# Token softmax sums as single rows, inverses spread over the partitions through DRAM, rows through Wo two segments late

## The chip, the cores and the metric

One core of a Trainium2 chip runs the whole program. The metric is device time in microseconds of one launch, inputs and outputs as the reference has them. Several runs are given by their median; the profile is one further execution, taken by the hardware profiler.

## The reference, cut to what matters

Four blocks follow each other: A, B, A, B, each added to the residual `x` of 2048 x 512. B is a gated MLP with a 2048 x 2048 mixing over tokens. A is a recurrent attention over 64 segments of 32 tokens, and it is where the change is:

```python
mem = mem0                                   # 8 rows
for s in range(n_seg):                       # 64 segments, 32 tokens each
    h = concatenate([mem, x_segment])        # 40 rows of 512
    q, k, v = (einsum('btd,dhe->bhte', h, W) for W in (Wq, Wk, Wv))   # 32 heads of 128
    scores = where(mask, q @ k.T * 128**-0.5, -1e9)
    o = softmax(scores) @ v
    o = einsum('bhte,hed->btd', o, Wo)
    mem = o[:, :8]                           # the next segment starts from these 8 rows
    outs.append(o[:, 8:])                    # 32 token rows
```

So the eight memory rows of a segment must have gone through projection, attention and Wo before the next segment's projections can begin. The 32 token rows of a segment are wanted by nothing in that loop.

## The kernel before

**Tiling.** The heads are put on the free side. Q and K are projected in two halves `r` of 16 heads, by matrix multiplications with only 32 stationary columns (the segment's 32 rows), four of which run side by side in the four 32-column groups of the array. Scores and their exponentials `E` are held as keys on partitions (two groups `g` of 64, in two variants per half `r`) and head and query on the free axis. The product with V (`pv`) then gives the output transposed, 128 channels on partitions, which is the stationary form that Wo needs.

**Softmax sums.** The exponentials are not divided. `pv` gives undivided outputs in `psO[r]`; the sums over keys come from multiplications with a matrix of ones, which puts each sum on all 128 partitions. `sums_ahead` and `sums_memory` do it for the 8 memory queries, `sums_tokens` for the 32 token queries into `psT`, 1024 numbers on each partition. ScalarE turns sums into inverses by Ln and Exp(-x). VectorE multiplies, straight from PSUM: `memory_out` for the memory queries, `tok_out` and `last_out` for the tokens.

**Wo with rows of two segments.** The stationary tile `uT` has 32 rows for each head: 24 token rows of the segment before and 8 memory rows of this one. `tok_out` writes 24 token rows of segment s into the `uT` of s+1; `last_out` keeps the last 8 in `oB`, which pass Wo later in a batch (`y_part`). `wo_pairs` writes into `px` (heads 0 to 17), `wo_rest` into `pw`, a corner of `psO[0]` (heads 18 to 31). `fold` and `build_hA` add them and transpose the memory rows into `hT` of the next segment; `store_o` stores the 24 token rows to `o_d`. After the last segment a final pass through Wo (L1290 to L1306) sends the rows that are still left.

**Order.** In A the order on TensorE, VectorE and ScalarE is the order of the source, written out by hand; each of these engines works strictly in that order. SyncE and GpSimd are ordered by a scheduler. TensorE's order in one segment, without what hides it:

```python
qk(0) qk(2) qk(1) qk(3) v_mm(0) scores(0) v_mm(1) scores(1)
fill() sums_ahead fill() pv(0) pv(1) sums_memory(1) sums_tokens
wo_pairs wo_rest fill()
```

`fill()` asks the generator `more` for one piece of work that is not part of the recurrence: `b_units` (projections of the last 8 rows of the next block's segments, six chunks for each block of four segments, cut into pieces of one, three and four k-tiles) or `y_part`. In the fourth segment of the first blocks there is none left. `run(copies)`, `run(turns)` and `run(adds)` issue what evicts such a piece. `prep_segment` copies small operands of a coming segment on GpSimd. `HALVED` gives for each segment how many k-tiles of `qk(3)`, `v_mm(0)` and `v_mm(1)` are issued as two matrix multiplications of 256 columns instead of one of 512.

**Buffers.** `att` is one PSUM tile of two banks, used in turn for `psQ`, `psS` and `psT`; `accA` holds the pieces, `accB` in turn `psm`, `psV`, `px`; `attO[0]` in turn `psK` and `psO[0]`, `attO[1]` is `psO[1]`.

Of the kernel before, what the change touches and what calls it, by code (L numbers as in the profile page):

```python
# [7 lines left out]
BF16 = mybir.dt.bfloat16  # L8
# [23 lines left out]
    "7900906005096002908070807070807080708070807080707080708070708071",  # L32
    "9060050968093111918080708070807070807070807080708070807080707080",
# [25 lines left out]
def _consts(ctx, tc, c, b_sp):  # L59
# [38 lines left out]
    for g in range(2):  # L98
        nc.vector.memset(half[64 * g:64 * g + 64, g, :], 1.0)
    bsp_bf = cp.tile([P, 16], BF16, name="bsp_bf")  # L100
# [8 lines left out]
    c.update(ident_bf=ident_bf, maskN=maskN, ones=ones, half=half)  # L109
# [380 lines left out]
def kernel(  # L490
# [32 lines left out]
    rows.vb_d = dram.tile([P, 8 * DH], BF16, name="vb_d")  # L523
    with tc.manual_schedule(engines=ORDERED):
# [148 lines left out]
def a_block(tc, c, rows, front, MV_in, RS_in, MV_out, RS_out, ahead, wo, S, first):  # L673
# [4 lines left out]
    maskN, ones, half = c["maskN"], c["ones"], c["half"]  # L678

    with ExitStack() as ctx:  # L680
# [14 lines left out]
        vsp = ctx.enter_context(tc.tile_pool(name="a_vs", bufs=2))  # L695
# [47 lines left out]
        KAr = [pers.tile([P, 2, 16, 32], BF16, name=f"KA{i}") for i in range(2)]  # L743
# [21 lines left out]
        copies, turns, adds = [], [], []  # L765
# [5 lines left out]
        def b_units(tb, early=0):  # L771
# [59 lines left out]
        def y_part(G, q, last=False):  # L831
# [9 lines left out]
            for k, _ in enumerate(wo_last(parts, pwB, last and q > 0)):  # L841
                if k in (0, 3):
                    yield
# [75 lines left out]
        def store_o(s, pw, t1):  # L919

            o_sb = wk.tile([P, P], F32, name="o_sb", bufs=1)
            nc.vector.tensor_tensor(out=o_sb[:], in0=pw, in1=t1[:], op=ALU.add)
            nc.sync.dma_start(o_d[SEG * (s - 1):SEG * s, :].rearrange("r (cg c) -> cg r c", cg=4), o_sb[:])

        def segment(s, fill, spare0, spare1, spare2, spare3, tail, loads):
# [3 lines left out]
            KA = KAr[s % 2]  # L929
# [75 lines left out]

            def sums_tokens(ps):
# [25 lines left out]
            def rview(r, lo, hi):  # L1032
                return Rt[:].rearrange("p g (r n q) -> p r g n q", r=2, q=32)[:, r, :, :, lo:hi]

# [6 lines left out]
            def tok_out(r):  # L1041
                nc.vector.tensor_tensor(out=hview(uT_nxt[:], r, 0, 24), in0=oview(r, 8, 32), in1=rview(r, 0, 24), op=ALU.mult)  # L1042

            def last_out(r):
                nc.vector.tensor_tensor(out=hview(oB, r, 8 * (s % 16), 8 * (s % 16) + 8), in0=oview(r, 32, 40), in1=rview(r, 24, 32), op=ALU.mult)

            psQ = att.tile([P, 2, 512], F32, name="psQ")
            r0, _, read = qk(0, psQ[:, 0, :])
            r2, mms, _ = qk(2, psQ[:, 1, :])
            other_bank(mms, read)  # L1050
# [26 lines left out]
            spare0()  # L1077

# [5 lines left out]
            Rt = segp.tile([P, 2, 512], F32, name="Rt", tag="Rt", bufs=1)  # L1084

            def token_factors(rs):
                nc.scalar.activation(out=Rt[:], in_=psT[:], func=ACT.Ln)  # L1087
                for r in rs:
                    rt = Rt[:, :, 256 * r:256 * r + 256]
                    nc.scalar.activation(out=rt, in_=rt, func=ACT.Exp, scale=-1.0)  # L1090
# [20 lines left out]
            sums_tokens(psT)  # L1111
            if ends_here:
                spare2()
                token_factors((1, 0))
            else:
                memory_out(1, sums[1])
            run(copies)
# [15 lines left out]
            if not ends_here:  # L1133
                token_factors((0, 1))
                run(turns)
                spare2()
            t1 = wk.tile([P, P], F32, name="t1", bufs=1)
            fold(px, cross, t1, None if ends_here else beside)
            if ends_here:
                fill()  # L1140
                for r in (1, 0):
                    tok_out(r)
                    last_out(r)
            if s + 1 < NSEG:
                build_hA(s + 1, pw, t1)
            if s > 0:
# [17 lines left out]
        if first:  # L1164
# [3 lines left out]
            for gen in (units, units1, units):  # L1168
                for _ in range(3):
# [15 lines left out]
        def values():  # L1185
            for u, n in ((units, 2), (units, 1), (units1, 2), (units1, 1), (units1, 2), (units1, 1)):
# [103 lines left out]
        ends = (uT[NSEG % 2], oBs[NB // 4 - 1][:, :, 96:128])  # L1290
        pw = accB.tile([P, 512], F32, name="pw")
        for n in range(H // 2):
            i = (n + H // 4) % (H // 2)
            for k in range(4):
                h = 2 * i + k % 2
                nc.tensor.matmul(pw[32 * k:32 * k + 32, :], lhsT=ends[k // 2][:, h, :], rhs=wo.head(h).rearrange("p (kt g el) -> p g kt el", kt=4, g=4),
                                 start=(n == 0), stop=(n == H // 2 - 1), tile_position=(0, 32 * k))
        o_sb = segp.tile([P, DM], F32, name="o_end", tag="Rt", bufs=1)
        nc.scalar.copy(o_sb[:], pw[:])
        for k in range(2):  # L1300
            o = o_sb[64 * k:64 * k + 32, :]
            nc.vector.tensor_tensor(out=o, in0=pw[64 * k:64 * k + 32, :], in1=o_sb[64 * k + 32:64 * k + 64, :], op=ALU.add)
            if k == 0:
                nc.gpsimd.dma_start(o_d[S - SEG:S - 8, :], o[0:24, :])
            else:
                nc.sync.dma_start(o_d[S - P:S, :].rearrange("(j r) c -> j r c", j=4)[:, 24:32, :], o)  # L1306
# [37 lines left out]
```

## Time and profile before

| | |
|---|---|
| runs (three) | 1616.52, 1618.78, 1620.8 us; median 1618.78 us |
| the profiled execution | 1620.98 us, span from the first to the last instruction 1619.3 us |
| granted TensorE clock | 0.997 |
| TensorE busy | 1572.9 us, 97% |
| VectorE busy | 1215.1 us, 75% |
| ScalarE busy | 1064.7 us, 66% |
| GpSimd busy | 286.4 us, 18% |
| A blocks | 29 to 690 us, 831 to 1482 us |

A line of the timeline has the start in us, the time until the end of the last instruction merged into it, engine, line, operation, output<-inputs, shapes and count; an idle time of the engine before it stands in brackets with what ended it. Ends of matrix multiplications are modelled, so a run of them is read by the distance of starts. A line of groups has count, then busy us, mean ns of one, then idle us of the engine before them and who ended it.

### The profile page before, as it was taken

The page shows a single profiled execution, that of the slowest core. Times are in us where ns is not written, and L with a number is a line of the kernel's source. Part 1 is how long each engine was busy: PE and PEld are TensorE (multiplying, and loading weights), DVE is VectorE, ACT ScalarE, POOL GpSimd, SP SyncE. Part 2 cuts the span into 40 slices and gives each one's busy share as a digit, 9 for nine tenths or more (in the row PEclk, how much of TensorE's full clock was granted, in tenths as well). Part 3 has the DMA queues.
Part 4 walks back from the last instruction along what each step waited for, and adds up shares of the span by engine and source line. Part 5 has one row for each costly group of instructions (what it writes and reads, how often), then busy time and mean ns, then how long its engine had stood idle before and what let it go on. Part 6 is the DMA issues. An engine that isn't in the chain of part 4 may idle for free.

```text
span 1619.3 us, 94188 instructions
## 1 busy us (share of the span) xinstructions
PE 1572.9 (97%) x42526; PEld 1000.3 (62%) x42526; DVE 1215.1 (75%) x3181; ACT 1064.7 (66%) x2277; POOL 286.4 (18%) x604
## 2 busy tenths in 40 slices
PE   5899999999999999999999999999999999999999
PEld 2566666666666666666656666666666666665565
DVE  4787777878888887884467777777888788877722
ACT  3677777777777777661047777777777777776400
POOL 5111111112211221320011111111121112214000
PEclk8999999999999999999999999999999999999999
DMA  9222122223322343297952221222333233526698
GB/s 370 68 44 45 45 43 44 44 43 81 85 47 44 86 92 72 88 189 151 212 168 50 49 47 47 47 47 47 73 90 72 48 73 92 88 62 174 141 190 170
DMA packets 261851, 148.44 MB, mean 92 GB/s; under 512 B 196425, under 2 KB 238001, under 8 KB 261449
## 3 DMA queue, kind: packets, MB, share of 16 engines
q1 hardware_dynamic: 248184, 98.59, 28.9%
q0 software_dynamic: 12976, 42.77, 8.7%
q8 instruction: 333, 5.46, 1.5%
q10 hardware_dynamic: 288, 1.05, 0.2%
q14 instruction: 70, 0.57, 0.1%
HBM read 59.42 MB, written 36.93 MB: 60 GB/s over the span
## 4 chain that ended last, share of the span: by engine, by line
PE 90%; DMA 4%; DVE 3%; ACT 1%; issue 1%; POOL 0%; SPq 0%; DVEq 0%
PE psQ L731 13%; PE psK L731 13%; PE psb L731 9%; PE pg L398 9%; PE px L808 9%; PE psm L731 7%; PE psV L731 6%; PE psO L815 6%; PE pz L298 3%; PE psO L1020 3%; PE pwB L827 3%; PE py L441 3%; PE psT L1012 2%; PE psS L968 2%; PE psO L1003 1%; PE psO L1023 1%
## 5 line engine op out<-in xcount | busy, mean ns | idle before, releaser
L731 PEld LDWEIGHTS <-hT 128*32 128x32 bf16 x14172 | 372.6, 96 | 284.6 <-DVE hT L917 65.5
L945 DVE STREAM_TRANSPOSE QQ<-rows 128x512 bf16<-128x512 bf16 x256 | 179.7, 702 | 19.5 <-ACT rows L942 11.9
L945 DVE STREAM_TRANSPOSE KA<-rows 128x512 bf16<-128x512 bf16 x256 | 176.4, 689 | 13.1 <-ACT rows L942 12.4
L398 PE MATMUL pg<-z,wspT 128*128 128x344 bf16 x1024 | 154.3, 309 | 0.0
L942 ACT CAST rows<-psQ 128x512 bf16<-128x512 f32 x256 | 142.2, 584 | 17.8 <-PE psQ L731 16.8
L1042 DVE TENSOR_TENSOR uT<-psO,Rt 128x384 bf16<-128x384 f32 x256 | 141.5, 553 | 13.6 <-ACT Rt L1090 5.9
L1090 ACT ACTIVATE Rt<-Rt 128x512 f32<-128x512 f32 x256 | 147.2, 622 | 4.1
L977 ACT ACTIVATE S<-psS 128x224 bf16<-128x224 f32 x256 | 91.4, 357 | 84.6 <-PE psS L972 84.6
L731 PE MATMUL psQ<-Wq_sb,hT 128*32 128x512 bf16 x2048 | 135.4, 381 | 9.0 <-ACT Rt L1087 6.3
L1039 DVE TENSOR_TENSOR uT<-psO,Rm 128x128 bf16<-128x128 f32 x252 | 73.4, 291 | 93.3 <-ACT Rm L1038 50.4
L808 PEld LDWEIGHTS <-uT 128*32 128x32 bf16 x4608 | 111.6, 96 | 47.2 <-DVE uT L1039 33.7
L808 PE MATMUL px<-Wo,uT 128*32 128x256 bf16 x3840 | 134.5, 274 | 2.1 <-DVE uT L1039 1.9
L731 PE MATMUL psV<-Wv_sb,hT 128*32 128x256 bf16 (+1 forms) x2420 | 134.3, 346 | 1.5 <-issue 1.5
L731 PE MATMUL psQ<-Wk_sb,hT 128*32 128x512 bf16 x2048 | 134.9, 381 | 0.0
L1087 ACT ACTIVATE Rt<-psT 128x1024 f32<-128x1024 f32 x128 | 131.0, 1024 | 5.5 <-PE psT L1012 2.5
L731 PE MATMUL psK<-Wk_sb,hT 128*32 128x512 bf16 (+1 forms) x2832 | 134.6, 320 | 0.0
L731 PE MATMUL psK<-Wv_sb,hT 128*32 128x512 bf16 (+1 forms) x2776 | 134.5, 323 | 0.0
L731 PE MATMUL psm<-Wq_sb,hT 128*32 128x512 bf16 x2048 | 134.1, 379 | 0.0
L398 PEld LDWEIGHTS <-wspT 128*128 128x128 bf16 x1024 | 100.1, 98 | 53.2
L815 PE MATMUL psO<-Wo_high,uT 128*32 128x128 bf16 x7168 | 123.7, 219 | 2.5 <-DMA Wo_high<-in_A_Wo_dram 2.5
L900 POOL COPY KX<-old 128x128 bf16<-128x128 bf16 x128 | 68.2, 549 | 320.8 <-PE psS L972 247.0
L900 POOL COPY KX<-front 128x128 bf16<-128x128 bf16 x126 | 64.5, 540 | 310.8 <-PE psS L972 247.3
(203 smaller groups left out, 2911.1 us busy)
## 6 DMA issues: line engine op xcount, KB each, us to landing
o_d<-o_sb SPq DMA_DIRECT2D x126, 64.0 KB
vb_d<-front SPq DMA_DIRECT2D x29, 256.0 KB
VX<-vb_d SPq DMA_DIRECT2D x116, 64.0 KB
ln_x<-xd SPq DMA_DIRECT2D x26, 256.0 KB
y_o<-o_d POOLq DMA_DIRECT2D x22, 256.0 KB, 3.9
xd<-y_o POOLq DMA_DIRECT2D x22, 256.0 KB, 2.7
Wk_sb<-in_A_Wk_dram POOLq DMA_DIRECT2D x8, 512.0 KB, 10.0
Wv_sb<-in_A_Wv_dram POOLq DMA_DIRECT2D x8, 512.0 KB, 11.3
```

The costliest lines, as they stand in the source:

```text
L398: nc.tensor.matmul(pg[t][:, k, 0:344], lhsT=wsp[t][:, st, :], rhs=z(st, 344 * k, 344 * k + 344), start=(st == 0), stop=(st == NT - 1))
L731: mms.append(nc.tensor.matmul(ps[32 * cg:32 * cg + 32, n * k:n * k + n], lhsT=lhs(kt, cg), rhs=r[:, m * k:m * k + m], start=(kt == 0), sto ...
L808: nc.tensor.matmul(px[at:at + 32, 0:256], lhsT=lhs[:, h, :], rhs=wo_rhs(h, slice(k + 2, None, -2) if h % 2 else slice(k, None, 2)), start= ...
L815: nc.tensor.matmul(pw[32 * cg:32 * cg + 32, :], lhsT=lhs[:, h, :], rhs=wo_rhs(h, cg), start=False, stop=(h == H - 1), tile_position=(0, 32 ...
L900: eng.tensor_copy(KX[:, :, r].rearrange("p g (k i) -> p i g k", i=4), bs["KTB"][:, r].rearrange("p (i g) k -> p i g k", i=4)[:, :, :, 8 * ...
L942: return r, mms, nc.scalar.copy(r[:], ps)
L945: nc.vector.transpose(out=QQ[:, j % 2, :, 0:32] if j < 2 else KA[:, j % 2], in_=r[:])
L977: return nc.scalar.activation(out=S[:, r], in_=psS[:, r, 0:224], func=ACT.Exp, scale=scale)
L1039: nc.vector.tensor_tensor(out=hview(uT_cur[:], r, 24, 32), in0=oview(r, 0, 8), in1=rm.rearrange("p g (n q) -> p g n q", q=8), op=ALU.mult)
L1042: nc.vector.tensor_tensor(out=hview(uT_nxt[:], r, 0, 24), in0=oview(r, 8, 32), in1=rview(r, 0, 24), op=ALU.mult)
L1087: nc.scalar.activation(out=Rt[:], in_=psT[:], func=ACT.Ln)
L1090: nc.scalar.activation(out=rt, in_=rt, func=ACT.Exp, scale=-1.0)
```

## The change

Sums. `sums_tokens` (four multiplications by ones, results on all partitions, 512 and 128 columns) is used in the last segment alone. Elsewhere `sums_rows` multiplies by `pick`, 32 stationary columns, 16 for each key group: eight multiplications of 128 and 32 columns in the four column groups, and each sum stands on 16 equal partitions of `psT[:, 0, 0:128]`. `row_factors` makes inverses of these 128 columns by Ln and Exp on ScalarE, into `Rr`, and four small DMAs write eight rows of 512 bytes of it to DRAM (`r_d`). At the end of the segment `spread_r` loads these 4 KB to each of the 128 partitions of `Rt`.

Outputs. The undivided outputs of segment s are copied by ScalarE from `psO` to `raw` in two halves (`raw_out`), in segment s+1 right behind the casts of `qk(0)` and `qk(2)`. VectorE multiplies `raw` by `Rt` near the end of segment s+1 (`divide`, where `tok_out` and `last_out` stood), into the `uT` of s+2 and into `oB`. So token rows pass Wo two segments late, and the final pass through Wo has three groups of rows instead of two.

Pieces. There are four `fill()` in each segment instead of three; the new one stands behind `sums_rows`, ahead of `wo_pairs`. The chunks are cut into pieces of one, two, one and four k-tiles. `HALVED` has new numbers; the tiles `KA` and `VA` have one buffer instead of two.

```diff
-    "7900906005096002908070807070807080708070807080707080708070708071",
-    "9060050968093111918080708070807070807070807080708070807080707080",
+    "0750909190919191906060506060506050606050606050605060605060605070",
+    "0091909190919091907050606050606050605060605060605060506060506070",
...
-                for kts in (((0,), (1, 2, 3)), ((0, 1, 2, 3),))[k % 2]:
+                for kts in (((0,), (1, 2), (3,)), ((0, 1, 2, 3),))[k % 2]:
...
+        def divide(s, u, r):
+            n = slice(16 * r, 16 * r + 16)
+            oB = oBs[s // 16]
+            for o, lo, hi in ((u[:, n, 0:24], 0, 24), (oB[:, n, 8 * (s % 16):8 * (s % 16) + 8], 24, 32)):
+                nc.vector.tensor_tensor(out=o, in0=raw[:, n, lo:hi], in1=Rt[:, n, lo:hi], op=ALU.mult)
+
+        def spread_r(s):
+            nc.sync.dma_start(Rt[:].rearrange("p h q -> p (h q)"), rows.r_d[s % 2][:].rearrange("a c -> (a c)").partition_broadcast(P))
...
+            def sums_rows(ps):
+                for k in range(2):
+                    for q in range(4):
+                        e = E[:, q // 2, q % 2, :]
+                        rhs = e[:, 160:224].rearrange("p (i b e) -> p i b e", i=4, b=2)[:, :, 1, :] if k else heads40(e[:, 0:160])[:, :, 8:40]
+                        o = ps[32 * q:32 * q + 32, :].rearrange("p (i q) -> p i q", i=4)
+                        nc.tensor.matmul(o[:, :, 24:32] if k else o, lhsT=pick[:].rearrange("p g m -> p (g m)"), rhs=rhs,
+                                         start=(k == 0), stop=True, tile_position=(0, 32 * q), skip_group_check=True)
...
+            def raw_out(r):
+                nc.scalar.copy(raw[:].rearrange("p (r g n) q -> p r g n q", r=2, g=2)[:, r], oview(r, 8, 40))
...
             r0, _, read = qk(0, psQ[:, 0, :])
+            run(late[0:1])
             r2, mms, _ = qk(2, psQ[:, 1, :])
+            run(late[1:2])
...
+            def row_factors():
+                Rr = segp.tile([P, P], F32, name="Rr", bufs=1)
+                nc.scalar.activation(out=Rr[:], in_=psT[:, 0, 0:P], func=ACT.Ln)
+                nc.scalar.activation(out=Rr[:], in_=Rr[:], func=ACT.Exp, scale=-1.0)
+                for r in range(2):
+                    for g in range(2):
+                        nc.sync.dma_start(rows.r_d[s % 2][4 * r + 2 * g:4 * r + 2 * g + 2, :],
+                                          Rr[64 * r:64 * r + 64, :].rearrange("(a b) c -> a b c", b=32)[:, 16 * g, :])
...
-            sums_tokens(psT)
...
+                sums_rows(psT[:, 0, 0:P])
                 memory_out(1, sums[1])
+                row_factors()
+            if not (first and s == 0):
+                fill()
             run(copies)
...
             if not ends_here:
-                token_factors((0, 1))
                 run(turns)
...
             if not ends_here:
-                tok_out(0)
-                last_out(0)
+                if s > 0:
+                    divide(s - 1, uT_nxt, 0)
                 fill()
             run(copies)
             if not ends_here:
-                tok_out(1)
-                last_out(1)
+                if s > 0:
+                    divide(s - 1, uT_nxt, 1)
+                spread_r(s)
+                late.extend((lambda: raw_out(0), lambda: raw_out(1)))
```

The last segment keeps `sums_tokens`, `token_factors` and multiplication straight from PSUM (`direct_out`); the final pass through Wo is 24 steps of four multiplications of 512 columns instead of 16, with one eviction for each third of the fourth column group.

More of the change, by code (lines that the diff above doesn't have):

```diff
@@ L108, in _consts @@
     tctx.close()
-    c.update(ident_bf=ident_bf, maskN=maskN, ones=ones, half=half)
+    c.update(ident_bf=ident_bf, maskN=maskN, ones=ones, half=half, pick=pick)
     return c
@@ L523 @@
     rows.vb_d = dram.tile([P, 8 * DH], BF16, name="vb_d")
+    rows.r_d = [dram.tile([8, P], F32, name=f"r_d{i}") for i in range(2)]
     with tc.manual_schedule(engines=ORDERED):
@@ L677, in a_block @@
     scale = float(DH) ** -0.5
-    maskN, ones, half = c["maskN"], c["ones"], c["half"]
+    maskN, ones, half, pick = c["maskN"], c["ones"], c["half"], c["pick"]
     with ExitStack() as ctx:
@@ L742, in a_block @@
         NKQ = 2
[L743 removed]
+        KA = pers.tile([P, 2, 16, 32], BF16, name="KA")
+        raw = pers.tile([P, H, 32], F32, name="raw")
+        Rt = pers.tile([P, H, 32], F32, name="Rt")
         QQr = [pers.tile([P, 2, 16, 40], BF16, name=f"QQ{i}") for i in range(NKQ)]
@@ L1110, in segment @@
                 sums_memory(1, sums[1])
-            sums_tokens(psT)
             if ends_here:
+                sums_tokens(psT)
                 spare2()
@@ L1168, in a_block @@
             for gen in (units, units1, units):
-                for _ in range(3):
+                for _ in range(4):
                     next(gen)
@@ L1289, in a_block @@
         y_norm(NB - 5, nc.sync, rowp.tile([P, DM], BF16, name="rows", tag="rowsQK", bufs=3)[:])
-        ends = (uT[NSEG % 2], oBs[NB // 4 - 1][:, :, 96:128])
+        ends = (uT[NSEG % 2], QQr[NSEG % NKQ][:].rearrange("p r n q -> p (r n) q")[:, :, 0:32], oBs[NB // 4 - 1][:, :, 96:128])
         pw = accB.tile([P, 512], F32, name="pw")
[L1292 to L1306, printed above, removed]
+        o_sb = raw[:].rearrange("p h q -> p (h q)")[:, 0:DM]
@@ new lines, in a_block @@
+        for q, beside in enumerate((lambda: attO[1].tile([P, 2, 512], F32, name="pw0")[:, 1, :], lambda: accA.tile([P, 512], F32, name="pw1")[:], lambda: pw[:])):
+            last = beside()
+            for k in range(8):
+                n = 8 * q + k
+                for i in range(4):
+                    src, h, o = (ends[i], (n + 16) % 24, pw[:]) if i < 3 else (ends[q], 24 + k, last)
+                    nc.tensor.matmul(o[32 * i:32 * i + 32, :], lhsT=src[:, h, :] if src is not ends[0] else src[:, h, 0:32],
+                                     rhs=wo.head(h).rearrange("p (kt g el) -> p g kt el", kt=4, g=4),
+                                     start=((n if i < 3 else k) == 0), stop=((n if i < 3 else k) == (23 if i < 3 else 7)),
+                                     tile_position=(0, 32 * i), skip_group_check=True)
+            nc.scalar.copy(o_sb[32 * q:32 * q + 32, :], last[96:128, :])
@@ L1307, in a_block @@
+        nc.vector.tensor_tensor(out=o_sb[0:96, :], in0=pw[0:96, :], in1=o_sb[0:96, :], op=ALU.add)
+        nc.gpsimd.dma_start(o_d[S - 2 * SEG:S - SEG - 8, :], o_sb[0:24, :])
+        nc.gpsimd.dma_start(o_d[S - SEG:S - 8, :], o_sb[32:56, :])
+        nc.sync.dma_start(o_d[S - P:S, :].rearrange("(j r) c -> j r c", j=4)[:, 24:32, :], o_sb[64:96, :])
         run(copies)
```

42 lines of the change are left out of this document (23 added, 19 removed).

## The prediction

> **What bounds the kernel now.** I read the page first: shares by engine and the chain that ended last.
>
> ```profile
> PE 1572.9 (97%) x42526; PEld 1000.3 (62%) x42526; DVE 1215.1 (75%) x3181; ACT 1064.7 (66%) x2277; POOL 286.4 (18%) x604
> ...
> PE 90%; DMA 4%; DVE 3%; ACT 1%; issue 1%; POOL 0%; SPq 0%; DVEq 0%
> ```
>
> TensorE is 97% busy and holds 90% of the chain, so a faster ScalarE or VectorE gives nothing by itself. I therefore went to the timeline of TensorE, for one segment with pieces and one without. A segment runs from one `psQ` to the next. First a segment with pieces (the columns are start, time to the end of the last, line, tiles, count):
>
> ```profile
> 311.46 1.04 PE L731 MATMUL psQ<-Wq_sb,hT 128*32 128x512 bf16 x16
> ...
> 316.90 0.39 PE L827 MATMUL pwB<-Wo_high,front 128*32 128x512 bf16 x4
> 317.12 0.29 PE L1003 MATMUL psO<-E,half 128*32 128x64 bf16 x16
> 317.23 0.82 PE L827 MATMUL pwB<-Wo_high,front 128*32 128x512 bf16 x12
> 317.99 0.32 PE L1020 MATMUL psO<-E,VA 64*128 64x80 bf16 x8
> ...
> 318.20 0.31 PE L1020 MATMUL psO<-E,VA 64*128 64x80 bf16 x8
> ...
> 318.40 0.22 PE L994 MATMUL psO<-E,ones 64*128 64x64 bf16 x4
> 318.46 0.44 PE L1012 MATMUL psT<-E,ones 64*128 64x512 bf16 x4
> 318.82 1.05 PE L808 MATMUL px<-Wo,uT 128*32 128x256 bf16 x30
> ...
> 319.81 0.96 PE L815 MATMUL psO<-Wo_high,uT 128*32 128x128 bf16 x56
> 320.60 1.04 PE L827 MATMUL pwB<-Wo_high,front 128*32 128x512 bf16 x16
> 321.46 1.23 PE L731 MATMUL psQ<-Wq_sb,hT 128*32 128x512 bf16 x16
> ```
>
> The period is 321.46 - 311.46 = 10.00 us and TensorE starts something all the time. `sums_tokens` (L1012) holds it from 318.46 to 318.82: 0.36 us. Now a segment without pieces, TensorE and then VectorE:
>
> ```profile
> 191.48 1.04 PE L731 MATMUL psQ<-Wq_sb,hT 128*32 128x512 bf16 x16
> ...
> 198.06 0.32 PE L1020 MATMUL psO<-E,VA 64*128 64x80 bf16 x8 [0.41 <-DVE E L980]
> ...
> 198.27 0.22 PE L994 MATMUL psO<-E,ones 64*128 64x64 bf16 x4
> 198.33 0.44 PE L1012 MATMUL psT<-E,ones 64*128 64x512 bf16 x4
> 198.70 1.05 PE L808 MATMUL px<-Wo,uT 128*32 128x256 bf16 x30
> ...
> 201.28 1.05 PE L731 MATMUL psQ<-Wq_sb,hT 128*32 128x512 bf16 x16 [0.63 <-ACT Rt L1087]
> ```
> ```profile
> 197.63 0.38 DVE L980 TENSOR_TENSOR E<-S,maskN 128x448 bf16<-128x448 bf16 x1
> ...
> 199.22 0.29 DVE L1039 TENSOR_TENSOR uT<-psO,Rm 128x128 bf16<-128x128 f32 x1 [0.49 <-ACT Rm L1038]
> ```
>
> Here 1.73 us of pieces are missing (four-column-group steps of 0.216 us: 16 multiplications take 0.865 us, 320.60 to 321.46), yet the period is 9.80 us. So two bounds lie close together: TensorE's own work, about 10.0, and the recurrence, 9.8. In the recurrence the second `pv` starts 198.06 - 191.48 = 6.58 after `psQ`, right behind the second masked exponentials (L980 ends at 6.53), against 6.74 with pieces; and the memory rows of half 1 reach `uT` at 199.51, or 8.03. Whatever TensorE saves, at most 0.2 us of a segment can come out.
>
> How many segments are of which kind I take from the starts of `psQ` (this group, 16 for each of 128 segments):
>
> ```profile
> L731 PE MATMUL psQ<-Wq_sb,hT 128*32 128x512 bf16 x2048 | 135.4, 381 | 9.0 <-ACT Rt L1087 6.3 <-DVE hT L217 1.7 <-DVE hT L917 0.7
> ```
>
> Of 125 periods (without the first of all and the two block ends) 9 are below 9.95, 39 above 10.05 (12 us beyond 10.01 in sum; late VectorE work and waits for DMA), 77 between.
>
> **TensorE's part of the change.** Out goes the slot of 0.36 us. In come eight `sums_rows` multiplications, four side by side. The nearest row is `sums_ahead` (L1003), of the same 32-column form: 16 in 317.12 to 317.23, 7 ns each, bound by 64 columns; with 128 and 32 columns I estimate 0.08 us, plus 0.1 for the change from 64-row to 32-column form that now comes ahead of it. That 0.1 is seen where the forms change now: the piece at 317.23 has three steps of 0.216 and so ends at 317.88, `pv` starts at 317.99. Bounds: 0.12 to 0.25. The Trainium skill (TensorEngine Tiling (Array Packing), Instruction Overhead) gives each multiplication some 60 cycles of overhead, which speaks against many short ones; by it eight cost 0.2 us and nearly all the saving is gone. The L1003 row, 7 ns each, disagrees, so I go by the row. So 0.18 us replace 0.36.
>
> The pieces hold the same work; 0.216 us of them moves from ahead of the first `pv` to behind `sums_rows`. That pulls `pv` forward into the second bound. In us from `psQ`: the first `pv` could start at 6.53 - 0.22 = 6.31, the second at 6.52, but L980 allows 6.58. From there `pv` 0.20, `sums_memory` 0.06, change and `sums_rows` 0.18, piece 0.22: `px` at 7.25 instead of 318.82 - 311.46 = 7.36. Heads from 16 on are reached 0.88 later (16 of 18 heads of 0.99 us), at 8.13, after `uT`'s 8.03. So a common segment gains 0.11, not 0.18: period 9.89. Without a piece behind `sums_rows`, `px` would wait for 8.03 and gain nothing, as the segments without pieces will (9.78, from 9.80).
>
> **ScalarE's part.** Its groups before:
>
> ```profile
> L1087 ACT ACTIVATE Rt<-psT 128x1024 f32<-128x1024 f32 x128 | 131.0, 1024 | 5.5 <-PE psT L1012 2.5
> ...
> L1090 ACT ACTIVATE Rt<-Rt 128x512 f32<-128x512 f32 x256 | 147.2, 622 | 4.1
> ...
> L1038 ACT ACTIVATE Rm<-Rm 128x128 f32<-128x128 f32 x252 | 78.1, 310 | 7.9
> ```
>
> Out: 1.02 + 2 x 0.62 = 2.27 us of a segment. In: Ln and Exp of 128 columns, 0.31 each at most, and two copies of 512 from PSUM, near a cast's 0.58 each: 1.78 us. That saves 0.5 us of an engine that does not bind; what counts is the place. Two places may hurt.
>
> First, the copies stand between the casts that the transposes wait for.
>
> ```profile
> 403.25 1.04 PE L731 MATMUL psQ<-Wq_sb,hT 128*32 128x512 bf16 x16
> ```
> ```profile
> 404.34 0.58 ACT L942 CAST rows<-psQ 128x512 bf16<-128x512 f32 x1
> ...
> 406.94 0.59 ACT L942 CAST rows<-psK 128x512 bf16<-128x512 f32 x1 [0.29 <-PE psK L731]
> ...
> 313.34 1.05 ACT L942 CAST rows<-psQ 128x512 bf16<-128x512 f32 x2
> ```
>
> The four casts are ready at 1.09, 1.95, 2.81 and 3.69 after `psQ`. Two back to back take 1.05, so they follow each other at 0.47. Then: cast 1.09, copy 1.56, cast 2.03, copy 2.50, cast 2.97, and the fourth at 3.69, on time. At the full 0.58 each the fourth starts at 3.99; that is a rival below. The copies also add waits. Each must not overwrite `raw` before `divide` has read that half: VectorE is through `store_o` some 0.4 after `psQ`, and two multiplications take 0.76 (0.47 apart, the last 0.28), so the halves are free at about 1.2 and 1.9, ahead of 1.56 and 2.50. Were it later, the casts of K and of the second Q half would stand behind it. And `psK` takes the bank of half 0 at 2.6; that copy ends at 2.1. The single `KA` and `VA` are rewritten 2.7 and 5 after `psQ`, when their readers of the segment before are long done: nothing.
>
> Second, the row inverses now stand ahead of a piece's cast and of the copy that `fold` waits for.
>
> ```profile
> 309.19 0.57 ACT L793 CAST rowsB<-psb 128x512 bf16<-128x512 f32 x1
> 310.04 0.26 ACT L1132 COPY cross<-px 64x128 f32<-64x128 f32 x1 [0.29 <-PE px L808]
> ```
>
> The copy has 0.29 us of idle time in front; 0.53 (Ln, Exp) come in, and `px` ends 0.11 earlier. It is about 0.14 to 0.2 late, against 0.1 between `fold` and the second half of Wo and 0.05 between `hT` and `psQ`. I take 0.01 in the common case (9.90) and 0.1 for the bound.
>
> **VectorE, SyncE, DMA.** Two multiplications of 384 and two of 128 from SBUF replace the same from PSUM.
>
> ```profile
> L1042 DVE TENSOR_TENSOR uT<-psO,Rt 128x384 bf16<-128x384 f32 x256 | 141.5, 553 | 13.6 <-ACT Rt L1090 5.9
> ...
> L240 DVE TENSOR_TENSOR y_o<-y_o,y_x 128x256 f32<-128x256 f32 x32 | 14.5, 452 | 3.7 <-DMA y_o<-o_d 3.4
> ```
>
> L240, from SBUF, costs what 553 for 384 lets expect of 256 (some 420): no change, and the waits for `Rt` at this place (5.9 us in all) go.
>
> ```profile
> o_d<-o_sb SPq DMA_DIRECT2D x126, 64.0 KB
> ...
> y_o<-o_d POOLq DMA_DIRECT2D x22, 256.0 KB, 3.9
> ...
> Wk_sb<-in_A_Wk_dram POOLq DMA_DIRECT2D x8, 512.0 KB, 10.0
> ```
>
> SyncE issues five DMAs more in each segment, some 0.5 us each. Ahead of `spread_r` its queue holds the four stores, a transpose or two and `o_d`: about 5.5 us from the inverses at 8.2, so `spread_r` issues near 13.9, which is 3.9 of the next segment. Behind its waits stand transposes wanted a segment later. Its 512 KB lands after 3.9 (256 KB) to 10.0 us (512 KB while all weights load); I take 4.5, nearer to the first because this load runs alone. Then `Rt` is there at 8.9 and `divide` wants it at 10.35: free, with 1.4 us to spare.
>
> **Block ends.** Eight steps more through Wo, 8 x 0.216 = 1.73 us. B's first projections take 0.67 of it, which they wait there now:
>
> ```profile
> 695.25 4.81 PE L298 MATMUL pz<-front 128*128 128x512 bf16 x24 [0.67 <-ACT z L299]
> ```
>
> 1.06 each, 2.1 us for both blocks.
>
> **Sum.** 77 x 0.11 = 8.5; for the 39 long segments, where VectorE or a DMA ends last, I take 0.08, 3.1; the 9 without pieces 0.2: 11.8 us, less 2.1, is 9.7. The profiled execution of 1620.98 us (span 1619.3) becomes 1611.3; it stands 2.2 above the median of the runs, 1618.78, so the forecast is 1609.1 us.
>
> **Rivals.**
> 1. *The gain is hidden anyway.* The fold's copy is late by its bound, 0.1, in the three of four segments whose piece ends at that place; 0.11 shrinks to 0.01 there. For it: only 0.29 idle time. Against: 0.1 of slack in two places. Left: a quarter of 8.5 + 3.1, less 2.1: 1618 us. Chance 0.13. A `sums_rows` of 0.2 us would end here too (`px` at 7.37); that is the skill's overhead rule again, and with L1003 against it I give it 0.02 of the 0.13.
> 2. *Slower: the copies push the casts.* At 0.58 each the fourth cast is 0.3 late; the second masked exponentials, 0.05 ahead of `pv`, then move by 0.2 (0.1 is slack in the transposes), the period is 10.10. Decides from a fourth cast later than about 3.8. For it: strided source, float output, later still where statistics stand in front. Against: the spacing of 0.47. 116 x 0.09 + 2.1 = 12.5: 1631 us. Chance 0.15. `spread_r` landing after 6 us would end there too, through `divide` ahead of the transposes: 0.07 more.
> 3. *TensorE's bound alone counts.* The exponentials come earlier because ScalarE has less to do, `pv` doesn't wait: 0.18 for 116 segments, less 2.1: 1600 us. For it: VectorE no longer waits for `Rt`. Against: L980 follows from the projection of V, not from that. Chance 0.1.
>
> **How the numbers follow.** Forecast 0.55, rivals 0.13, 0.22, 0.1. Under 0.3% (4.9 us) no difference can be measured here. Faster: forecast and third, 0.65, of which 0.02 goes to the same: 0.63; same 0.13 + 0.02 = 0.15; slower 0.22. The range reaches from just below the third case to where most of the slower cases begin (0.16 of them left out, and 0.04 below): 1599 to 1627.
>
> **What would show it.** Right: `sums_rows` in under 0.1 us; the second `pv` near 6.6 with a wait for L980; `px` near 7.25; periods of 9.9; the four casts at unchanged times; no wait of VectorE for the load of `Rt`. Wrong: `px` still at 7.36, a late fourth cast, `divide` waiting for a DMA, or the copy for `fold` ending its wait by ScalarE.

## The result, and the profile after

The changed kernel takes 1691.2 us (median of four runs, 1684.8 to 1694.1), the kernel before 1618.5: a ratio of 1.0443, with a 95% interval of 1.0410 to 1.0477. It is 73 us slower where 9.7 us less were forecast. The profiled execution of after took 1684.8 us (span 1683.1, granted clock 0.993), 64 us more than that of before; the readings below are about these 64.

From the page of after: busy time, two DMA queues, HBM, and the chain.

```profile
PE 1591.1 (95%) x42847; PEld 1023.2 (61%) x42870; DVE 1208.1 (72%) x3180; ACT 979.0 (58%) x2407; POOL 288.5 (17%) x606
...
q1 hardware_dynamic: 268080, 165.05, 39.0%
...
q8 instruction: 335, 5.49, 1.3%
...
HBM read 125.48 MB, written 37.41 MB: 97 GB/s over the span
...
PE 85%; DMA 6%; DVE 4%; issue 3%; ACT 2%; POOL 1%; SPq 0%; DVEq 0%; ACTq 0%; POOLq 0%
```

The same two rows of before:

```profile
q1 hardware_dynamic: 248184, 98.59, 28.9%
...
HBM read 59.42 MB, written 36.93 MB: 60 GB/s over the span
```

TensorE's share of the chain went from 90% to 85%, DMA's from 4% to 6%, "issue" from 1% to 3%. So the place to look is a wait that TensorE didn't have before. First, though, a segment of after that nothing disturbs, TensorE's timeline:

```profile
261.86 0.32 PE L1045 MATMUL psO<-E,VA 64*128 64x80 bf16 x8
...
262.06 0.22 PE L1009 MATMUL psO<-E,ones 64*128 64x64 bf16 x4
262.22 0.26 PE L1028 MATMUL psT<-E,pick 128*32 128x128 bf16 x8
262.31 0.39 PE L736 MATMUL psb<-Wq_sb,hB 128*32 128x512 bf16 x4
262.53 1.04 PE L824 MATMUL px<-Wo,uT 128*32 128x256 bf16 x30
...
264.29 1.04 PE L736 MATMUL psb<-Wk_sb,hB 128*32 128x512 bf16 x16
265.20 0.62 PE L736 MATMUL psQ<-Wq_sb,hT 128*32 128x512 bf16 x8
```

This segment's `psQ` starts at 255.26. The second `pv` is at 6.60, `sums_rows` takes 0.09 (262.22 to 262.31), `px` starts at 7.27 and the period is 9.94: the steps of the prediction, to a few hundredths. Now the waits of TensorE over the whole run (total, times, longest):

```profile
PE px L824 <- DVE uT L1061: 10.5, 7, 2.6
PE px L824 <- issue: 9.4, 16, 2.5
PE pz L302 <- ACT z L303: 7.2, 2, 4.2
PE psO L1048 <- issue: 4.2, 7, 1.0
PE psQ L736 <- issue: 3.7, 8, 1.2
PE pw L1342 <- DVE yB L862: 3.5, 2, 1.8
PE psO L1045 <- issue: 3.5, 5, 0.9
```

Rows "<- issue" are idle times at which nothing that the profile shows was missing: with the smaller rows, 53 of them over 0.1 us, 25.9 us in sum, against 7 with 2.3 us before, where these two rows hold the longer ones:

```profile
PE psV L731 <- issue: 1.5, 2, 0.8
...
PE px L808 <- issue: 0.5, 2, 0.3
```

An idle time is counted from the modelled end of the multiplication before it, and one under 0.1 us not at all, so the 25.9 us are rather too little than too much. One of the 53, in a segment that takes 11.31 us:

```profile
638.84 0.31 PE L1045 MATMUL psO<-E,VA 64*128 64x80 bf16 x7 [0.18 <-DVE E L995]
640.05 0.19 PE L1045 MATMUL psO<-E,VA 64*128 64x80 bf16 x1 [0.91 <-issue]
```

The eighth of eight equal multiplications, with its data long there, comes 0.91 us late. What it lacked was the instruction itself. TensorE has 42847 + 42870 = 85717 records of multiplications and weight loads; divided by 256 that is 334.8, and the instruction queue q8 moved 335 packets of 16 KB. If the 209 records of TensorE's sequencer (semaphores) are counted too, all 53 idle times stand at one and the same record number modulo 256 (it drifts from 194 to 182 over the run, probably as records are missing), and TensorE resumes 1.2 to 1.7 us after the end of a q8 packet. They are waits for a page of 256 instructions, an instruction page below.

The broadcast load stands beside these waits. Its 128 packets of 4 KB keep moving for some 2.6 us of each segment. With the boundaries of the instruction pages placed by that record number, its packets were moving in the first 1.0 us of the instruction page before the wait, when the next one is to be fetched, in 41 of the 53 cases; of the 281 other instruction pages only 95 had this. In e4_before_dma, below, it is 41 of 47 against 80 of 285.

By the starts of `psQ` the 63.8 us lie in two places: 46.8 in the 124 inner segments of the two A blocks (1251.8 to 1298.7 us), 17.2 in the two stretches from the start of the last segment of A to the next A block or the end (306.1 to 323.3). Each was then tested.

### The profile page after: what moved, and what is told of

It reads as the page before. It is cut to its first block, busy times and chain, and to the rows that moved or that the text cites. A ratio compares the mean times of both kernels' runs of the same rounds, so it can differ in the third digit from the quotient of the medians.

```text
span 1683.1 us, 95905 instructions
## 1 busy us (share of the span) xinstructions
PE 1591.1 (95%) x42847; PEld 1023.2 (61%) x42870; DVE 1208.1 (72%) x3180; ACT 979.0 (58%) x2407; POOL 288.5 (17%) x606
## 4 chain that ended last, share of the span: by engine, by line
PE 85%; DMA 6%; DVE 4%; issue 3%; ACT 2%; POOL 1%; SPq 0%; DVEq 0%; ACTq 0%; POOLq 0%
PE psQ L736 13%; PE psK L736 12%; PE pg L402 9%; PE psb L736 8%; PE px L824 8%; PE psm L736 6%; PE psO L831 6%; PE psV L736 6%; PE pz L302 4%; PE psO L1045 3%; PE py L445 2%; PE pwB L843 2%; DMA y_o<-o_d 2%; PE psS L983 1%; PE psT L1028 1%
## 5 line engine op out<-in xcount | busy, mean ns | idle before, releaser
L957 ACT CAST rows<-psQ 128x512 bf16<-128x512 f32 x256 | 152.1, 594 | 118.2 <-PE psQ L736 111.3
L960 DVE STREAM_TRANSPOSE KA<-rows 128x512 bf16<-128x512 bf16 x256 | 180.3, 704 | 23.1 <-ACT rows L957 22.1
L736 PE MATMUL psQ<-Wq_sb,hT 128*32 128x512 bf16 x2048 | 141.8, 383 | 16.7 <-DVE hT L933 7.3
L1064 ACT COPY raw<-psO 128x512 f32<-128x512 f32 x252 | 152.4, 605 | 0.3 <-DVE old L778 0.3
L824 PE MATMUL px<-Wo,uT 128*32 128x256 bf16 x3840 | 135.8, 274 | 15.5 <-DVE uT L1061 10.5
L824 PEld LDWEIGHTS <-uT 128*32 128x32 bf16 x4608 | 121.4, 96 | 43.1 <-DVE uT L1061 17.4
L736 PE MATMUL psm<-Wq_sb,hT 128*32 128x512 bf16 x2048 | 137.9, 380 | 0.0
L736 PE MATMUL psK<-Wv_sb,hT 128*32 128x256 bf16 (+1 forms) x2736 | 137.7, 325 | 0.0
L736 PE MATMUL psV<-Wv_sb,hT 128*32 128x512 bf16 (+1 forms) x2244 | 135.7, 360 | 1.7 <-issue 1.7
L778 DVE TENSOR_TENSOR uT<-raw,Rt 128x384 bf16<-128x384 f32 x252 | 136.5, 542 | 0.0
L809 ACT CAST rowsB<-psb 128x512 bf16<-128x512 f32 x124 | 71.5, 577 | 86.5 <-PE psb L736 85.8
```

Of the source, the lines that this page charges most:

```text
L736: mms.append(nc.tensor.matmul(ps[32 * cg:32 * cg + 32, n * k:n * k + n], lhsT=lhs(kt, cg), rhs=r[:, m * k:m * k + m], start=(kt == 0), sto ...
L778: nc.vector.tensor_tensor(out=o, in0=raw[:, n, lo:hi], in1=Rt[:, n, lo:hi], op=ALU.mult)
L809: nc.scalar.copy(r, ps)
L824: nc.tensor.matmul(px[at:at + 32, 0:256], lhsT=lhs[:, h, :], rhs=wo_rhs(h, slice(k + 2, None, -2) if h % 2 else slice(k, None, 2)), start= ...
L957: return r, mms, nc.scalar.copy(r[:], ps)
L960: nc.vector.transpose(out=QQ[:, j % 2, :, 0:32] if j < 2 else KA[:, j % 2], in_=r[:])
```

## The experiments

Theory 1: the 64 MB of the broadcast load delay instruction pages and other loads. Theory 2: the new order of instructions puts page boundaries where the instructions are dense. Theory 3: the five DMAs hold up what stands behind them in SyncE's queue. Ratios are to the kernel before, with 95% intervals; "segments" and "ends" are the two sums of the section above.

| kernel | us | ratio | segments | ends | TensorE by issue |
|---|---|---|---|---|---|
| before | 1618.5 | 1 | 1251.8 | 306.1 | 2.3 |
| after | 1691.2 | 1.0443 (1.0410 to 1.0477) | 1298.7 | 323.3 | 25.9 |
| e1_narrow | 1654.1 | 1.0221 (1.0195 to 1.0247) | 1271.8 | 324.7 | 11.6 |
| e2_no_dma | 1640.6 | 1.0137 (1.0118 to 1.0156) | 1251.2 | 326.3 | 4.2 |
| e3_bf16 | 1670.0 | 1.0331 (1.0292 to 1.0370) | 1282.2 | 323.4 | 15.4 |
| e4_before_dma | 1679.7 | 1.0379 (1.0355 to 1.0403) | 1303.7 | 306.4 | 35.4 |
| e5_ends | 1676.3 | 1.0346 (1.0319 to 1.0374) | 1296.6 | 311.5 | 22.4 |
| e6_shift | 1622.4 | 1.0020 (1.0006 to 1.0034) | 1254.6 | 304.8 | 4.6 |
| e7_pool | 1741.6 | 1.0763 (1.0721 to 1.0804) | 1335.7 | 337.4 | 38.0 |
| e8_stores | 1643.0 | 1.0141 (1.0121 to 1.0162) | 1253.1 | 323.0 | 2.6 |
| e9_pool_stores | 1715.2 | 1.0580 (1.0527 to 1.0634) | 1312.3 | 341.9 | 41.0 |
| e10_y_later | 1689.6 | 1.0429 (1.0393 to 1.0466) | 1295.8 | 326.4 | 33.0 |
| e11_all | 1666.1 | 1.0288 (1.0259 to 1.0317) | 1274.2 | 331.3 | 21.5 |
| e12_no_dma_ends | 1626.6 | 1.0044 (1.0029 to 1.0059) | 1251.8 | 312.8 | 4.2 |
| e13_act_stores | 1708.6 | 1.0548 (1.0526 to 1.0570) | 1318.0 | 326.6 | 29.4 |
| e15_bf16_ends | 1653.2 | 1.0211 (1.0185 to 1.0236) | 1273.7 | 314.7 | 13.2 |

**e1_narrow: the load without its bytes.**

```diff
-nc.sync.dma_start(Rt[:].rearrange("p h q -> p (h q)"), rows.r_d[s % 2][:].rearrange("a c -> (a c)").partition_broadcast(P))
+nc.sync.dma_start(Rt[:].rearrange("p h q -> p (h q)")[:, 0:16], rows.r_d[s % 2][:].rearrange("a c -> (a c)")[0:16].partition_broadcast(P))
```

> The changed kernel (1691 us), but the load of the inverses brings only 16 numbers (64 bytes) to each partition instead of 1024 (4 KB); the rest of Rt stays at zero, so the token rows are left undivided or zero. The four stores, the load's place in SyncE's queue and its waits stay. Theory 1, the 64 MB of loaded bytes delay TensorE's instruction pages and other loads: about 1612 to 1625 us, and TensorE's idle time by issue (25.9 us in the changed kernel) back under 8 us. Theory 2, the new instruction order puts the page boundaries badly: 1685 to 1695. Theory 3, the five DMAs in SyncE's queue hold up what stands behind them: 1680 to 1695.

37 of the 73 us go with the bytes, though the place in the queue, its waits and the 128 packets are the same. Theories 2 and 3 expected 1680 and more. But 1654.1 is above the 1612 to 1625 of theory 1, and 11.6 us of waits by issue stay instead of under 8: a part of the loss does not come with the bytes.

**e2_no_dma and e8_stores: no load; no stores either in e2.** The call of `spread_r` is taken out, in e2_no_dma the four `dma_start` of `row_factors` too.

> The changed kernel without the four stores and the load (Rt stays at zero, so token rows are lost); ScalarE still makes the inverses, VectorE still multiplies. Theory 1 (bytes): as with the narrow load, 1608 to 1620 us. Theory 2 (page boundaries): 1685 to 1695. Theory 3 (SyncE's queue): 1608 to 1620, well below the narrow load. The prediction's own sum without its DMA term, 1609, is tested here too: periods of 9.89 to 9.95 in nearly all segments with pieces.

> The changed kernel with the four stores of the inverses in each segment, but no load (Rt stays at zero, so token rows are lost). Without any of these DMAs it was 1640.6 us, with the stores and a load of 64 bytes to each partition 1654.1. If the stores (504 DMAs of 1 KB) make the 13.5 us: 1650 to 1656. If the load does, by its 128 small packets or by SyncE waiting for it: 1639 to 1645.

Without the DMAs the segments cost what they cost before (1251.2), in the order of instructions of the change, and the waits by issue are 4.2 us. So all 47 us of the segments come from the DMAs, and theory 2 falls here. By the run times, the DMAs cost 50.6 us: the stores alone make 2.4 of them, the load's 128 packets and its waits, which no run separates, 11 more, and the bytes the other 37. But 1640.6 is still 22 above before, and far from the 1608 to 1620 expected: this run separates the ends, which cost as much without the DMAs (326.3).

**e3_bf16: half the bytes.** `r_d`, `Rt` and the output of Exp in BF16 instead of F32.

> The changed kernel with the inverses in bfloat16 from Exp on: rows of 256 bytes in DRAM, 2 KB to each partition, half the bytes of the load. Theory 1: about half of the loss goes, 1640 to 1665 us. Theories 2 and 3: 1680 to 1695.

1670: 64 bytes, 2 KB and 4 KB to a partition cost 13.5, 29.4 and 50.6 us over e2_no_dma. The loss grows with the bytes, from 13.5 us at nearly none. The time is a little above the range of theory 1.

**e4_before_dma: the kernel before, with only the DMAs added.**

```diff
+                for i in range(4):
+                    nc.sync.dma_start(rows.r_d[s % 2][2 * i:2 * i + 2, :], Rt[2 * i:2 * i + 2, 0, 0:P])
...
+                nc.sync.dma_start(Dz[:].rearrange("p h q -> p (h q)"), rows.r_d[s % 2][:].rearrange("a c -> (a c)").partition_broadcast(P))
```

> The kernel before, with the DMAs of the change alone: four stores of 1 KB from its own Rt to DRAM and a load of 4 KB to each partition of an unused tile at the end of each segment (KA and VA with one buffer to make room). TensorE's order and page boundaries are those of before. Theory 1 and theory 3: 1665 to 1700 us. Theory 2: 1615 to 1622.

61 us slower, in the profile 52 and all of it in the segments, with an order of instructions that is otherwise that of before and a tile that nobody reads. Its waits of TensorE:

```profile
PE psO L817 <- issue: 21.0, 22, 1.3
...
PE psQ L732 <- issue: 5.1, 8, 1.2
PE px L810 <- issue: 3.1, 6, 1.0
```

L817 is `wo_rest`, the densest stretch of the segment. So the DMAs alone, in another order of instructions, make a loss of this size, 33 of the 52 us as waits by issue (35.4 against 2.3). This run can't tell theory 1 from theory 3; e1_narrow and e3_bf16 do that, where only the bytes change.

**e6_shift: other page boundaries, no DMA added.** One digit of `HALVED` for segment 2, 0 to 4.

> The kernel before (1618.5 us) with four k-tiles of segment 2 issued as halves: 16 multiplications more there, nothing else, no DMA added. All later boundaries of 256 instructions on TensorE fall 32 records earlier in the segments, so that the shortest stretch of 256 lasts 2.83 us instead of 3.41. Theory, a page of 256 instructions can't follow the one before it in under some 3.0 to 3.3 us (fetch starts 0.65 after the boundary, takes 0.97, is usable 1.4 later): 0.2 to 0.35 us for each pair of segments, 1630 to 1642 us, and TensorE idle by issue of 10 to 25 us instead of 2.3. Rival, the issue gaps come from something else than the position of the pages: 1617 to 1621.

1622.4: 3 us, not 12 to 24, and no more than six waits by issue. Instruction pages that last 2.83 us were mostly fetched in time as long as the broadcast was not there. My limit of 3.0 to 3.3 us was wrong, and theory 2 explains next to nothing.

**e7_pool, e9_pool_stores, e13_act_stores: other queues.** e7 issues the load, e9 the four stores by `nc.gpsimd`; e13 issues the stores by `nc.scalar` behind the copy to `cross`.

> The changed kernel with the load of the inverses issued by GpSimd instead of SyncE; bytes, packets and stores as in the change. Theory 1 (bytes on the DMA engines): 1678 to 1700 us, no great change, the load only starts earlier in the segment. Theory 3 (SyncE's queue held up behind the load's waits): 1640 to 1675.

> The changed kernel (1691 us) with the four small stores of the inverses issued by GpSimd; the load stays with SyncE, which has four issues of about 0.5 us less ahead of it and so starts the load earlier than now (3.4 to 4.75 us into the segment, its last packet at 7). Bytes and packets as in the change. Theory, what counts is whether the load lies ahead of a page that TensorE needs within 3.3 us (those asked for at 5.4 and at 7.1 of the segments): 1665 to 1682 us, TensorE's idle time by issue from 25.9 to under 15 us. Rival, only the amount counts, not the time within the segment: 1685 to 1697.

> The changed kernel (1691 us) with the four small stores issued by ScalarE, right behind the copy for the fold, where it stands idle until the casts of the next segment; the load stays with SyncE, which then has four issues less (2 us) ahead of it. This is to move the load earlier within the segment, which the stores on GpSimd did not do (its first packet stayed at 3.6 to 4.8 us). Theory, the time of the load against the pages that TensorE asks for at 5.4 and 7.1 us decides: first packet near 2.5 us, 1660 to 1682 us, TensorE idle by issue under 15 us. Rival, only the amount counts: 1685 to 1697. If four issues on ScalarE hold up the first cast: over 1700.

All three are slower than the change. Taking the load or the stores out of SyncE's queue did not bring the gain of theory 3 (1640 to 1675 in e7), so with e1_narrow it falls as the main cause. e7 and e9 also lie above every range that was expected, and e13 where late casts were to put it. Each pays for its queue. In e7 the load stands among GpSimd's `y_o` loads, and VectorE waits for these ahead of the memory rows (`uT`). In e9 VectorE waits 20.3 us for `Rt`, nearly all of it at the ends of the blocks, because the stores land late, and the waits by issue rise to 41.0 us. In e13 four issues take 2.16 us of ScalarE, so that the first cast is late. Rows of e7 (TensorE, then VectorE), of e9 (SyncE) and of e13 (ScalarE):

```profile
PE px L824 <- DVE uT L1061: 27.9, 12, 2.8
...
DVE y_o L244 <- DMA y_o<-o_d: 30.6, 12, 3.0
```
```profile
SPq L781 <- DMA r_d<-Rr: 204.4, 101, 42.4
```
```profile
250.10 2.16 ACTq L1176 DMA_DIRECT2D r_d<-Rr  x4
252.73 0.59 ACT L957 CAST rows<-psQ 128x512 bf16<-128x512 f32 x1 [2.42 <-PE psQ L736]
```

The second question, whether the time of the load within the segment matters, stays open: its first packet stood at 4.8 and 3.4 us (medians of even and odd segments) in the change, at 4.8 and 3.6 in e9 and at 4.1 and 3.8 in e13. None of them moved it far enough. With the same bytes and packets the waits by issue are 25.9 us in the change and 41.0 in e9, so the amount alone doesn't set them, and the counts of late instruction pages beside the load, given with the profile above, speak for its time; no run has tested that by itself.

**e5_ends: the ends of the blocks.**

```diff
-        o_sb = raw[:].rearrange("p h q -> p (h q)")[:, 0:DM]
+        o_sb = vsp.tile([P, 2, 4, DH], BF16, name="VA")[:].rearrange("p g i e -> p (g i e)").bitcast(F32)
...
-... lambda: accA.tile([P, 512], F32, name="pw1")[:], lambda: pw[:])):
+... lambda: attO[0].tile([P, 2, 512], F32, name="pw1")[:, 1, :], lambda: pw[:])):
```

> The changed kernel (1691 us) with two tiles exchanged in the final pass through Wo: the sums of the last rows go to the tile of VA instead of raw (raw lies where block B's first z tiles are written), and the second third of the fourth column group goes to the bank of psO[0] instead of accA. Theory, the ends of the blocks cost 10 us each because Wo waits 1.8 us for the last piece's fold in accA and B's first Gelu waits 4.5 to 5.7 us for the DMA that reads raw: both waits go, 1.9 + 2.4 us at the first block end and 1.9 + 3.5 at the second, about 1681 us. Rival, these waits stand in for others there: 1688 to 1692.

1676.3 us; the ends fall from 323.3 to 311.5, 12 us by two names of tiles. In the change, `accA` still held a piece whose fold VectorE did late, and B's first Gelu wrote into the place of `raw`, which a DMA to `o_d` was still reading. The run exchanges both tiles at once, so the 12 us are not split between them. TensorE and ScalarE of the change at the first end:

```profile
712.17 0.38 PE L1342 MATMUL pw<-Wo_high,QQ 128*32 128x512 bf16 x1 [1.78 <-DVE yB L862]
```
```profile
722.21 2.52 ACT L303 ACTIVATE z<-pz 128x1376 bf16<-128x1376 f32 x2 [4.52 <-DMA o_d<-raw]
```

Behind these waits the clock is lower too. From 720.1 to 723.5 us TensorE was busy for 0.43 us, and from 723.5 to 726.9 its granted clock was 0.50; at the second end the same happens from 1549.5. Each can cost at most half of its 3.4 us, and neither e5_ends nor e12 has one there.

**e12_no_dma_ends: without both losses.**

> The changed kernel without stores and load of the inverses (Rt stays at zero, token rows are lost), with the two tiles exchanged in the final pass through Wo: the change without both losses found so far. They were 50 and 15 us: 1625 to 1628 us. The prediction's sum without its DMA term was 1609; what is left above it (some 17 us) then lies in the steps of the segments that were to gain 0.1 each and in the block ends that were to cost 2.1 in all. Rival: the two losses overlap, 1630 to 1641.

1626.6, as expected; the two losses add up. It is still 0.44% slower than before (interval 0.29% to 0.59%), and 17 us above the forecast.

**e10_y_later, e11_all, e15_bf16_ends: what could be kept.** e10 takes each `y_o` one segment later, by a third state in the list `ys`; e11 has the edits of e3, e5, e9 and e10; e15 those of e3 and e5.

> The changed kernel with the addition to the rows y_o taken one segment later after their load (a 256 KB load of GpSimd's queue, one per block of rows), otherwise the same. Theory, the loads land late behind the broadcast and VectorE waits for them ahead of the memory rows of half 1: the 14.5 us of waiting for y_o and the 10.5 us that TensorE waits for uT go, 1678 to 1684 us. Rival, another wait stands behind at the same places: 1688 to 1693.

> All of it together: the changed kernel with inverses in bfloat16 (21 us less alone), the two tiles exchanged in the final pass through Wo (15 us less), the stores issued by GpSimd, and the rows y_o added one segment later. If the parts add up, with 8 us each for the last two: 1640 us; if they overlap, up to 1655. The kernel before is 1619; below it only if the load's cost goes entirely.

> The changed kernel with inverses in bfloat16 (half the bytes, 1670.0 us alone) and the two tiles exchanged in the final pass through Wo (1676.3 alone); the stores stay with SyncE and the rows y_o where the change has them. If the two losses add up, 1691 - 21 - 15 = 1655 us; then what made the version with all four edits 1666 was the stores on GpSimd. If not, 1662 to 1668.

e10 is a miss; its rival, another wait behind, came. VectorE's 14.5 us for `y_o` are gone, and with them the 10.5 us of TensorE behind `uT`, but the time hardly moves: the waits by issue are 33.0 instead of 25.9. A likely reading, not tested, is that a delay of TensorE gives its next instruction page time, so that where one goes the other comes up. e15 is the best version with the whole computation, 1653.2, where 1655 was expected from the sum. e11 missed its 1640 to 1655. It is 16.6 us above e15 in span, and all of that lies at the ends (331.3 against 314.7), in a wait that the stores on GpSimd bring, as in e9:

```profile
DVE uT L778 <- DMA Rt<-r_d: 17.8, 4, 7.6
```

No version beats the kernel before: even the one without any of the DMAs and with mended ends is slower.

## Why the prediction was wrong, step by step

- **What fails is the DMA step.** "Then `Rt` is there at 8.9 and `divide` wants it at 10.35: free" was right about `Rt`: no wait for it is among the large waits of after, and the load's last packet comes at 7 us, sooner than forecast. But it costs only when the load itself arrives. The step asked who waits for this transfer and not who shares the DMA engines with it. The load takes q1 from 28.9% to 39.0%, doubles what is read from HBM (59.4 to 125.5 MB), and TensorE's own instructions come by DMA too: 47 us in the segments, where I wrote 0. "This load runs alone" was the mistake; an instruction page is fetched every 5 us on average (335 in 1683 us), and `y_o` is loaded beside it. Of the 47 us, against e2_no_dma, 21.7 are idle times by issue (25.9 against 4.2) and 9.8 waits for `uT` behind late `y_o` loads (10.5 against 0.7); two stretches of 3.4 us at a granted clock of 0.50 (from 1249.1 and 1419.8) make at most 3.4. Some 12 us are not itemised.
- **TensorE's part** was right in the segment shown: `sums_rows` 0.09 us with 0.16 from `sums_memory` to its start, against 0.18 + 0.06; the second `pv` at 6.60 (forecast 6.58), `px` at 7.27 (7.25). The 0.2 us that the prediction works out for eight multiplications one after another did not come: they stand in two rounds of four side by side. The third rival doesn't come into it.
- **The fold's copy** was mis-sized. I took 0.01 in the common case and 0.1 as a bound. In the segment shown the last piece is done at 264.29 + 0.865 = 265.15 and `psQ` starts at 265.20; `fold` waits for ScalarE's copy, which stands behind the inverses and a piece's cast:

```profile
263.36 0.57 ACT L809 CAST rowsB<-psb 128x512 bf16<-128x512 f32 x1
263.95 0.26 ACT L1175 COPY cross<-px 64x128 f32<-64x128 f32 x1
```
```profile
264.24 0.29 DVE L925 TENSOR_TENSOR t<-px,cross 128x128 f32<-128x128 f32 x1 [0.23 <-ACT cross L1175]
```

  The sign named for this, a wait of `fold` that ScalarE ends, is there: over 0.15 us in 81 of 128 segments of e12, in none before. From the last multiplication of `wo_rest` to the next `psQ` it took 0.91 us before; in e12 it is still 0.91 (median) behind a `y_part` piece, and 0.96 to 1.01 where a piece is cast. So the term of 0.01 measures 0.05 to 0.1.

  Without the DMAs (e12) the medians of the first to the fourth segment of a block are 10.02, 9.94, 10.00 and 9.97, against 10.02, 10.00, 10.01 and 10.00 before: a gain of 0 to 0.06. Only segments with a `y_part` piece, which isn't cast there, reach the forecast 9.89, and only 7 of 28 of them. The first rival, "the gain is hidden anyway", describes most of this. Some more waits for instruction pages (4.2 us against 2.3) take part of what is left; together the 11.8 us forecast for the segments become 0. Their last 2 to 3 us I haven't itemised.
- **ScalarE's copies among the casts** were right: in the same segment they start at 1.10, 1.58, 2.06, 2.54, 3.01 and 3.69 after `psQ` (forecast 1.09, 1.56, 2.03, 2.50, 2.97, 3.69).

```profile
256.36 0.59 ACT L957 CAST rows<-psQ 128x512 bf16<-128x512 f32 x1 [0.64 <-PE psQ L736]
256.84 0.59 ACT L1064 COPY raw<-psO 128x512 f32<-128x512 f32 x1
257.32 0.60 ACT L957 CAST rows<-psQ 128x512 bf16<-128x512 f32 x1
257.80 0.62 ACT L1064 COPY raw<-psO 128x512 f32<-128x512 f32 x1
258.27 0.63 ACT L957 CAST rows<-psm 128x512 bf16<-128x512 f32 x1
258.95 0.58 ACT L957 CAST rows<-psK 128x512 bf16<-128x512 f32 x1
```

  The median of the fourth cast is 3.69 in all segments of after and of e12. In 28 of the 124 inner segments of e12 it comes later than 3.8: in 22 because TensorE itself writes `psK` late, in six because the copies stand behind statistics, so that it starts at 3.9 though `psK` is written at 3.7 (periods 10.08 to 10.19). So the slower rival, late casts, gave the right sign, but its mechanism happened in few segments and is not what makes the 73 us.
- **VectorE** was right: `divide` takes 542 ns for 384 columns, against 553 from PSUM.
- **The block ends** were mis-sized: 2.1 us forecast, 17.2 measured. The eight steps more cost their 1.73 us each time. Left out were the wait for `accA` and the one for the DMA that reads `raw` (12 us together, e5). Nor did B's projections absorb 0.67: they now wait for the third eviction, 1.5 us each in e12. The stretch at half clock behind the longer waits adds up to 1.7 us at each end.

Adding up: forecast -11.8 + 2.1 + 0; the profiles say 0 without the DMAs for the segments, + 17 at the ends, + 47 by the DMAs: 64.

## What to carry to other kernels

A DMA that nobody waits for isn't free: when TensorE runs at 97% with short instructions, as here, its instruction pages can be the transfers with the least slack. So price a new load by the bytes and packets it adds to the DMA engines, ask what else is fetched in the same stretch, and look for rows "<- issue" at a constant count of instructions. When a tile is given a second use at the end of a block, look which tile of the next block lies in its place, and whether a DMA still reads it. An operation put ahead of a copy with little slack costs that slack in the segments where a third operation already stands there.

## What the runs showed of the hardware

TensorE's instructions come in pages of 16 KB, 256 records, and it fetches one page ahead. In the kernel before, the fetch of an instruction page starts at a median of 0.65 us after the first instruction of the page before it ran and takes 1.1 us, and the first instruction of the page runs 1.2 us or more after the packet's end. With the broadcast the fetch takes 1.0 us but starts at 1.06 us, and at 1.76 for the 53 pages that TensorE waited for: it is the start that is late. What holds it back no run shows. The Trainium skill (Runtime: NRT & Kernel Launch, Instruction fetch mechanics) states blocks of 256 instructions that the sequencer fetches over its own DMA queue while it executes the current one, and calls the cost of crossing a boundary mostly hidden. The first part agrees with the 335 packets; the second holds for the kernel before (7 waits over 0.1 us, 2.3 us in all) and not beside 512 KB in each 10 us (47 waits and 35.4 us in e4_before_dma).

Not expected either: a load of only 64 bytes to each partition, 128 packets in a segment, costs 11 us more than none (e1_narrow against e8_stores), and four issues of 1 KB hold ScalarE for 2.16 us (e13_act_stores).

The granted clock falls behind a wait: in after, four windows of 3.4 us in which TensorE was busy for 0.03 to 1.61 us (up to 723.5, 1249.1, 1419.8 and 1549.5) are each followed by 3.4 us at 0.50 to 0.51. The kernel before has such a stretch only at its start and its end. In e7 and in the change these stretches, start and end included, add up to 67 and 26 us, so at most 21 of the 50 us between the two are of this kind.
